# Seven-product FFN: operand making in single steps, one placed behind each block product

## The chip, the cores and the metric

One core of one Trainium2 chip. The metric is the device time of one execution in microseconds, as the median of three runs. The core has TensorE (PE; its weight loads are PEld), VectorE (DVE), ScalarE (ACT), GpSimd (POOL) and SyncE (SP, which here only issues DMAs). Each engine works through its own queue in order.

## What is computed

Three stages in float32: a linear attention over `q`, `k`, `v` (8 x 8 heads, 576 positions, 64 wide), a mixture of eight experts on the 4608 x 512 result, and the feed-forward layer (FFN) that the change is about:

```python
def _moe2_ref(x, w1, w2, w3, w_out):          # x 4608 x 512, w1..w3 512 x 768, w_out 768 x 512
    h = np.maximum(np.maximum(x @ w1, x @ w2), x @ w3)
    return (h @ w_out).astype(np.float32)
```

## The kernel before, in words

The attention and the experts come first and end at about 640 us. The change leaves their work alone, but for the last expert block, in which the first weights of the FFN are made ready.

The FFN takes the tokens in 9 groups of 512. Its first layer makes, for each group, 9 *quads* (class `Quad`, made by `quad1`): three weight columns `fp` by three weights `j`, of which the maximum is taken. Its second layer makes 2 quads for each group (`quad2`). All 81 quads of the first layer run ahead of the 18 of the second. A quad is a 2 x 2 block product done with seven block products in place of eight (numbered 1 to 7; `Quad.step`). For each product both operands must be at hand: blocks of the raw tile as they are (products 1 to 4 on one side or the other) and sums and differences of them. *Sums* of one raw tile are four instructions (`sums_left`, `sums_right`) into a tile `sc`.

float32 runs on TensorE as three matmuls (`mm3`, L482 to L484): each operand is *split* into a high part and the rest (`split`, L797 and L798): ScalarE writes the high part, and VectorE, or in one case GpSimd, subtracts it from the source. A block product of the first layer has 2 x 3 matmuls of 256 columns, of the second 3 x 3. Making the operands of one raw tile is thus: sums (4 instructions), the *single* split (one block, 128 x 256), the *wide* split (two blocks, 128 x 512), and two *pair* splits of the sums (128 x 512 each). There are 9 raw tiles of w1 (a pair of operands for each quad of a group, kept for all groups), 3 of `w_out` (`w2_prep`), 3 of h for each group (`h_steps`, from DRAM), and two halves of x for each group, which first are transposed by TensorE (L1041) into PSUM tiles `tp`.

The order is written out by hand. The last loop runs over the quads n and over the products in the order 6(n), 4(n-1), 1(n+1), 5(n), 7(n), 2(n+1), 3(n); behind each product, `hook(n, p)` may emit other work into the engines' queues. What a product leaves in PSUM (`mm`, six buffers) is taken out at once in the order of emission: products 1, 6 and 5 by a ScalarE copy to `pu` (L1106), since the next product adds onto the same PSUM tile, the others by VectorE (L1091, L1093, L1094, L1116) or ScalarE (L1113) into `mt`. In `hook`:
- `w1_prep` (a generator, `w1_steps`) makes w1 ready from the last expert block on, one step per product; its single and wide splits have GpSimd for the subtraction;
- the operands of x for the next group are made behind four products of quads 6, 7 and 8 of the group;
- the operands of h for the next group are made all at once behind product 1 of the group's first quad: three single, three wide and six pair splits in a row.

Of the kernel before, what the change touches and what calls it, by code (L numbers as in the profile page):

```python
# [45 lines left out]
def kernel(  # L46
# [14 lines left out]
    rt_p = ctx.enter_context(tc.tile_pool(name="rt", bufs=1))  # L61
# [73 lines left out]
    stg_p = []  # L135
    wpools = []
# [369 lines left out]
    ec = ctx.enter_context(ExitStack())  # L506
    with ac:
# [11 lines left out]
        wpools.append(ctx.enter_context(tc.tile_pool(name="wa", bufs=NWA, side="right")))  # L519
        stg_p.append(ctx.enter_context(tc.tile_pool(name="stg", bufs=NSTG, side="right")))  # L520
# [303 lines left out]
    def operand_steps(raw, left, wide, single, whole, half, put, pool, eng=nc.vector):  # L824

        x = [[raw[:, a, b * 256 : (b + 1) * 256] for b in range(2)] for a in range(2)]
        sc = pool.tile([P, 4, 256], F32, name="sc")
        row, names = wide
        if left == "rows":
            sums_left(sc, x[0][0], x[0][1], x[1][0], x[1][1], nc.gpsimd)  # L830
        elif left == "cols":
            sums_left(sc, x[0][0], x[1][0], x[0][1], x[1][1], nc.gpsimd)
        else:
            sums_right(sc, x[0][0], x[0][1], x[1][0], x[1][1], nc.gpsimd)
        h = half()
        split(h, raw[:, 1 - row, single[0] * 256 : (single[0] + 1) * 256], eng)
        put(single[1], h)
        yield
        w = whole()
        split(w, raw[:, row], eng)  # L840
        put(names[0], w[:, :, 0:256])
        put(names[1], w[:, :, 256:])
        yield
        for c, (p, q) in ((0, (6, 7)), (2, (5, 3) if left else (5, 4))):
            w = whole()
            split(w, sc[:, c : c + 2].rearrange("p a b -> p (a b)"))
            put(p, w[:, :, 0:256])
            put(q, w[:, :, 256:])
            yield
# [10 lines left out]
    def w1_steps():  # L860
        half = halves(w1_tile)

        def load(p):
            while conv_done[0] < 2 * p + 2:
                next(conv)
            t = stg_p[0].tile([P, 2, 512], F32, name="stg")
            nc.sync.dma_start(out=t, in_=wfd[2 * p : 2 * p + 2].rearrange("i p c -> p i c"))
            return t

        nxt = load(0)  # L870
        for p in range(9):
            raw, nxt = nxt, load(p + 1) if p < 8 else None
# [151 lines left out]
    xt2_p = fx.enter_context(tc.tile_pool(name="xt2", bufs=18))  # L1024
# [12 lines left out]
    def f_xt(g, i, pool=ps_t, name="tp"):  # L1037
        for k in (i, i + 2):
            ps = pool.tile([P, 4, P], F32, name=name)
            for c in range(4):  # L1040
                nc.tensor.transpose(ps[:, c], xins[g, c // 2][:, c % 2, k * P : (k + 1) * P], ident)  # L1041
            xps[g, k] = ps.rearrange("p c t -> p (c t)")

    def x_new(g, *ps):
        for p in ps:
            for i in range(2):
                xops[g, p, i] = xt2_p.tile([P, 2, 256], F32R, name="xt2")
# [18 lines left out]
    def x_sum(g, n):
        p = (6, 7, 5, 4)[n]
        x_new(g, p)
        for i in range(2):
            x_put(g, p, i, xsc[g, i][:, n])  # L1070
# [93 lines left out]

    w2_half = halves(lambda: wb_p.tile([P, 2, 512], F32R, name="wB"))

    w2_raw = {}

    def w2_load(k):
        w2_raw[k] = stg_p[0].tile([P, 2, 512], F32, name="stg")  # L1170
        nc.sync.dma_start(out=w2_raw[k], in_=wfd[18 + k : 24 : 3].rearrange("i p c -> p i c"))

    def w2_prep(k):
        raw = w2_raw.pop(k)
        w2[k] = {}
        whole = lambda: wb_p.tile([P, 2, 512], F32R, name="wB")
# [247 lines left out]
```

## Time and profile before

| what | value |
|---|---|
| median of 3 runs | 1301.18 us (1300.61 to 1305.65) |
| the profiled execution | 1293.95 us, span 1292.2 us |
| PE busy | 1142.1 us (88%) |
| DVE busy | 833.9 us (65%) |
| ACT busy | 562.7 us (44%) |
| POOL busy | 329.1 us (25%) |
| granted TensorE clock, mean | 0.964 of 2.4 GHz |

The span is from the first to the last instruction. Busy shares are means over stages with different limits, so the stages are looked at by themselves. Where a row names a wait, as in `[3.12 <-ACT pu L1106]`, the engine stood idle for so many us until that instruction was done. A granted clock below 1.00 in a stretch is a mixture of the two levels 2.4 and 1.2 GHz.

### The profile page before, as it was taken

How to read it: one execution, taken by the hardware profiler on the slowest of the kernel's cores; microseconds unless marked ns; L12 is line 12 of the kernel's file. 1: busy time of each engine (PE TensorE's matmuls, PEld its weight loads, DVE VectorE, ACT ScalarE, POOL GpSimd, SP SyncE). 2: the span in 40 equal slices, each digit the busy share in tenths (PEclk: the TensorE clock that was granted, in tenths of full speed). 3: DMA queues.
4: the chain of work that ended last, by engine and by line, in shares of the span. 5: the costliest groups of instructions: out<-in, count | busy, mean ns of one | idle time of the engine just before them, and what ended most of it. 6: DMA issues, size and time to landing. Idle time of an engine off the chain costs nothing.

```text
span 1292.2 us, 34077 instructions
## 1 busy us (share of the span) xinstructions
PE 1142.1 (88%) x14212; PEld 1064.8 (82%) x14212; DVE 833.9 (65%) x1802; ACT 562.7 (44%) x1290; POOL 329.1 (25%) x376
## 2 busy tenths in 40 slices
PE   6999898988786999799878999999999999789886
PEld 6888787877675788688768999999999999678776
DVE  6889688788342677788676565565565668643551
ACT  4665555545431445565453332332332334343441
POOL 0001222204333464441663000000000005535530
PEclk9999999999877999899989999999999999899998
DMA  7576867568523666667421101101201113533411
GB/s 256 190 230 178 215 218 207 169 216 195 107 85 81 220 219 231 231 218 237 164 74 66 66 34 66 66 33 66 65 35 66 55 43 126 183 126 131 156 49 67
DMA packets 115470, 175.84 MB, mean 136 GB/s; under 512 B 20930, under 2 KB 58306, under 8 KB 115312
## 3 DMA queue, kind: packets, MB, share of 16 engines
q1 hardware_dynamic: 110592, 163.63, 39.8%
q0 software_dynamic: 4352, 8.71, 2.0%
q8 instruction: 113, 1.85, 0.6%
q10 hardware_dynamic: 368, 1.27, 0.3%
q14 instruction: 45, 0.37, 0.1%
HBM read 120.77 MB, written 54.78 MB: 136 GB/s over the span
## 4 chain that ended last, share of the span: by engine, by line
PE 59%; DMA 9%; DVE 9%; POOL 8%; issue 7%; ACT 6%; SPq 0%; POOLq 0%; DVEq 0%; ACTq 0%
PE mm L482 13%; PE mm L484 12%; PE mm L483 12%; PE kv L592 6%; PE n L632 5%; PE pr L552 5%; PE tr L569 3%; DMA list<-ids,idx 2%; ACT w L797 2%; DMA xb<-y,ixr 2%; POOL sq L201 1%; PE n L610 1%; PE tp L1041 1%; DMA xb<-y,ix0a 1%; POOL da L202 1%
## 5 line engine op out<-in xcount | busy, mean ns | idle before, releaser
L1106 ACT ACTIVATE pu<-mm 128x256 f32<-128x256 f32 x297 | 112.9, 382 | 244.4 <-PE mm L484 239.4
L482 PE MATMUL mm<-xt,w 128*128 128x256 f32 (+1 forms) x652 | 186.9, 287 | 7.4 <-ACT pu L1106 5.5
L483 PE MATMUL mm<-xt,w 128*128 128x256 f32 (+1 forms) x652 | 186.2, 286 | 1.7 <-DVE xt L478 0.9
L484 PE MATMUL mm<-xt,w 128*128 128x256 f32 (+1 forms) x652 | 186.2, 286 | 0.0
L482 PE MATMUL mm<-xt,wB 128*128 128x256 f32 x536 | 153.9, 287 | 4.0 <-ACT pu L1106 3.6
L483 PE MATMUL mm<-xt,wB 128*128 128x256 f32 x536 | 152.9, 285 | 1.1 <-DVE xt L478 1.1
L484 PE MATMUL mm<-xt,wB 128*128 128x256 f32 x536 | 152.5, 285 | 0.0
L1091 DVE TENSOR_TENSOR mt<-mm,pu 128x256 f32<-128x256 f32 x135 | 56.1, 421 | 121.8 <-PE mm L484 117.9
L482 PEld LDWEIGHTS mm<-xt,w 128*128 128x128 f32 x652 | 125.6, 193 | 8.9 <-ACT pu L1106 6.1
L483 PEld LDWEIGHTS mm<-xt,w 128*128 128x128 f32 x652 | 123.6, 190 | 2.3 <-DVE xt L478 1.2
L1093 DVE TENSOR_TENSOR pu<-mm,pu 128x256 f32<-128x256 f32 x162 | 68.1, 421 | 86.6 <-PE mm L484 86.6
L484 PEld LDWEIGHTS mm<-xt,w 128*128 128x128 f32 x652 | 123.6, 190 | 0.0
L801 POOL TENSOR_TENSOR sc<-stg 128x256 f32<-128x256 f32 x15 | 14.3, 954 | 408.0 <-DMA stg<-hd 377.9
L482 PEld LDWEIGHTS mm<-xt,wB 128*128 128x128 f32 x536 | 103.5, 193 | 5.0 <-ACT pu L1106 4.0
L592 PE MATMUL kv<-raw,e 128*64 128x74 f32 (+1 forms) x2560 | 96.9, 233 | 10.3 <-issue 10.0
L483 PEld LDWEIGHTS mm<-xt,wB 128*128 128x128 f32 x536 | 103.6, 193 | 1.8 <-DVE xt L478 1.8
L592 PEld LDWEIGHTS kv<-raw,e 128*64 128x64 f32 (+1 forms) x2560 | 83.3, 137 | 25.3 <-issue 23.8
L578 ACT ACTIVATE e<-d 128x512 f32<-128x512 f32 x144 | 82.7, 622 | 48.6 <-DVE d L559 46.9
L484 PEld LDWEIGHTS mm<-xt,wB 128*128 128x128 f32 x536 | 103.5, 193 | 0.0
L632 PE MATMUL n<-kvw,q 128*64 128x74 f32 x2304 | 97.0, 236 | 4.7 <-issue 4.0
L552 PE MATMUL pr<-wph,raw 64*64 64x128 f32 x2304 | 85.0, 285 | 12.0 <-DMA wph<-in_w_phi_dram 6.6
L557 DVE TENSOR_REDUCE m<-pr 128x8 f32<-128x1024 f32 x72 | 87.8, 1219 | 10.3 <-PE pr L552 9.3
(250 smaller groups left out, 2953.9 us busy)
## 6 DMA issues: line engine op xcount, KB each, us to landing
raw<-in_qkv_dram SPq DMA_DIRECT2D x46, 798.0 KB, 7.5
stg<-in_w_exp_dram SPq DMA_DIRECT2D x64, 512.0 KB, 5.1
hd<-mt SPq DMA_DIRECT2D x27, 512.0 KB, 3.4
pf<-in_w_ffn_dram SPq DMA_DIRECT2D x24, 512.0 KB, 5.2
hb<-hd SPq DMA_DIRECT2D x21, 512.0 KB, 5.1
xa<-xs SPq DMA_DIRECT2D x16, 576.0 KB, 5.1
xb<-xs SPq DMA_DIRECT2D x16, 576.0 KB, 6.0
stg<-xb SPq DMA_DIRECT2D x18, 512.0 KB, 5.4
```

What stands on the lines that cost most here:

```text
L482: nc.tensor.matmul(out=ps, lhsT=ah, rhs=bh, start=first, stop=False, skip_group_check=on)
L483: nc.tensor.matmul(out=ps, lhsT=ah, rhs=bl, start=False, stop=False, skip_group_check=on)
L484: nc.tensor.matmul(out=ps, lhsT=al, rhs=bh, start=False, stop=last, skip_group_check=on)
L552: nc.tensor.matmul(out=pr[p0 : p0 + 64, h, 2 * s + i], lhsT=raw[k0, o + p0 : o + p0 + 64], rhs=wph[k0], start=True, stop=True,)
L557: nc.vector.tensor_reduce(out=m, in_=pr, axis=AX.X, op=ALU.max, apply_absolute_value=True)
L569: nc.tensor.transpose(tr[:, 2 * h + i], d[:, h, i], ident)
L578: nc.scalar.activation(out=e[:, :, :, s], in_=ds[s2][:, :, 2:4], func=AF.Exp, scale=scale)
L592: nc.tensor.matmul(out=kvps[u, b][c : c + 64, 2 * h + s], lhsT=e[p0:p1, h, i, s, c : c + 64], rhs=v[p0:p1, h], start=t == 4 * b and h + s ...
L632: nc.tensor.matmul(out=ps[p0 : p0 + 64, i, h], lhsT=q[:, s, 2 * h + i, p0 : p0 + 64], rhs=kvw[u, b][:, 2 * h + s], start=s == 0, stop=s == 1,)
L1091: nc.vector.tensor_tensor(out=out, in0=ps, in1=tmp, op=ALU.add)
L1093: nc.vector.tensor_tensor(out=tmp, in0=ps, in1=tmp, op=ALU.add)
L1106: nc.scalar.activation(out=t, in_=ps, func=AF.Copy)
```

## The change

Operand making is cut into single steps: a class `Operands` with the methods `sums`, `single`, `wide`, `pair(0)` and `pair(2)` takes the place of the generator `operand_steps`, and a table `sched` says behind which product (quad n, position `at` in the order above) each step is emitted. `hook` and its conditions are gone.

```diff
-    def operand_steps(raw, left, wide, single, whole, half, put, pool, eng=nc.vector):
...
+    class Operands:
+        def __init__(self, raw, side, whole, half, sums, eng=nc.vector):
+            self.raw, self.side, self.whole, self.half, self.pool, self.eng = raw, side, whole, half, sums, eng
+            self.blocks = {}
+        def steps(self):
+            return [self.sums, self.single, self.wide, lambda: self.pair(0), lambda: self.pair(2)]
...
     def w1_steps():
-        nxt = load(0)
+        cur, nxt = load(0), None
+        yield
+        cur.sums()
         for p in range(9):
-            raw, nxt = nxt, load(p + 1) if p < 8 else None
+            nxt = load(p + 1) if p < 8 else None
             yield
             while w1_used[0] + 4 > (freed[0] - WF + NWA + NWB if not wc_p else NWA + NWB + NWC + 4):
                 yield
-            blocks = {}
-            for _ in operand_steps(raw, "rows", (0, (1, 2)), (1, 4), w1_tile, half, blocks.__setitem__, sc_p, nc.gpsimd):
+            for f in cur.steps()[1:]:
+                f()
                 yield
-            w1[p] = blocks
+                if f == cur.wide and nxt:
+                    nxt.sums()
+            w1[p] = cur.blocks
+            cur = nxt
...
-    xt2_p = fx.enter_context(tc.tile_pool(name="xt2", bufs=18))
+    xB_p = fx.enter_context(tc.tile_pool(name="xB", bufs=12))
+    xT_p = fx.enter_context(tc.tile_pool(name="xT", bufs=8))
...
+    def x_put(g, p, i):
+        if p in (1, 2, 3):
+            t = xB_p.tile([P, 2, 256], F32R, name="xB")
+            split(t, xps[g, i + 2 * (p > 1)][:, 256 * (p == 3) :][:, :256])
+        else:
+            t = xT_p.tile([P, 2, 256], F32R, name="xT")
+            split(t, xsc[g, i][:, (6, 7, 5, 4).index(p)])
+        xops[g, p, i] = t
+    def x_sums(g, i, part=(0, 1)):
+        a, b = xps[g, i], xps[g, i + 2]
+        sub = lambda o, x, y: nc.vector.tensor_tensor(out=o, in0=x, in1=y, op=ALU.subtract)
+        if 0 in part:
+            if g == groups[0]:
+                sc = mt_p.tile([P, 2, 512], F32, name="mt").rearrange("p a (b c) -> p (a b) c", b=2)
+            else:
+                sc = sc_p.tile([P, 4, 256], F32, name="sc")
+            xsc[g, i] = sc
+            nc.scalar.activation(out=sc[:, 3], in_=a[:, 256:], func=AF.Copy)
+            sub(sc[:, 2], sc[:, 3], a[:, 0:256])
+            sub(sc[:, 0], b[:, 256:], sc[:, 2])
+        if 1 in part:
+            sc = xsc[g, i]
+            sub(sc[:, 1], b[:, 256:], sc[:, 3])
+            sub(sc[:, 3], b[:, 0:256], sc[:, 0])
...
+    ORDER = (6, 4, 1, 5, 7, 2, 3)
+    def do(n, at, f, *args):
+        sched.setdefault((n, ORDER[at]), []).append((f, args))
...
+    def x_next(n0, g):
+        do(n0 + 3, 6, f_load, g)
+        for i in range(2):
+            q = n0 + 5 + i
+            do(q, 0, f_ps, g, i)
+            do(q, 0, f_xt, g, i)
+            for at, p in ((2, 1), (3, 2), (4, 3)):
+                do(q, at, x_put, g, p, i)
+            do(q, 5, x_sums, g, i, (0,))
+            do(q, 6, x_sums, g, i, (1,))
+        for i in range(2):
+            do(n0 + 8, 1 + i, x_put, g, 6, i)
+            do(n0 + 8, 4 + i, x_put, g, 5, i)
+            do(n0 + 8 + i, 6 * (1 - i), x_put, g, 7, i)
+            do(n0 + 9, 2 + i, x_put, g, 4, i)
...
+    def h_next(n0, i):
+        if i + 2 < NG:
+            for k in range(3):
+                do(n0, 1, h_load, groups[i + 2], k, hb_p, "hb", sb_p)
+        if i + 1 < NG:
+            g = groups[i + 1]
+            for k in range(3):
+                do(n0, 1, op_step, h_op, (g, k), 0)
+            at = [(n0 + (2 + t) // 7, (2 + t) % 7) for t in range(12)]
+            for s, first in ((1, 0), (2, 3), (3, 6), (4, 9)):
+                for k in range(3):
+                    do(*at[first + k], op_step, h_op, (g, k), s)
...
+    for n in range(5):
+        for at in range(7):
+            do(n, at, next, w1_prep, None)
+    do(5, 0, list, w1_prep)
...
-            hook(n, p)
+            for f, args in sched.pop((n, p), ()):
+                f(*args)
```

The steps for the second layer's first group (`to_layer2`) are placed one by one too: three tiles of h from quad 74 on, three of w_out from quad 77 to 80, where they were made a tile at a time behind quads 75 to 80. Besides: `sb` (sums of h) has 4 buffers and not 3; h is loaded two groups ahead and not three; pools are opened in another order, so that tiles lie at other addresses; the first x group is transposed in two halves, the two token halves of all its tiles one after the other, and its two loads stand behind four loads of w1 in SP's queue and not behind five.

On ScalarE in the second layer, from one copy `pu` (L1106, L1124 after) to the next but a group, there stood before:

```order
L1106 ACTIVATE pu<-mm 128x256 x2
L797 ACTIVATE w<-hb 128x256 x3
L797 ACTIVATE w<-hb 128x512 x3
L797 ACTIVATE w<-sc 128x512 x6
L1106 ACTIVATE pu<-mm 128x256
L1113 ACTIVATE mt<-mm 128x256
```

and there stand after:

```order
L795 ACTIVATE w<-hb 128x256
L1124 ACTIVATE pu<-mm 128x256
L795 ACTIVATE w<-hb 128x256 x2
L795 ACTIVATE w<-hb 128x512
L1131 ACTIVATE mt<-mm 128x256
L795 ACTIVATE w<-hb 128x512
L1124 ACTIVATE pu<-mm 128x256
L795 ACTIVATE w<-hb 128x512
L795 ACTIVATE w<-sc 128x512
L1124 ACTIVATE pu<-mm 128x256
L795 ACTIVATE w<-sc 128x512
L1124 ACTIVATE pu<-mm 128x256
```

The twelve splits that stood between two copies are dealt out between the copies of two quads.

On GpSimd at the start of the FFN, behind the last scatter of expert rows (`xb<-y`), before:

```order
L951 DMA xb<-y,ixr_8323 3456x512
L801 TENSOR_TENSOR sc<-stg 128x256
L802 TENSOR_TENSOR sc<-sc,stg 128x256
L803 TENSOR_TENSOR sc<-stg 128x256
L804 TENSOR_TENSOR sc<-stg,sc 128x256
L798 TENSOR_TENSOR w<-stg,w 128x256
L798 TENSOR_TENSOR wB<-stg,wB 128x512
```

and after:

```order
L802 TENSOR_TENSOR sc<-stg,sc 128x256
L966 DMA xb<-y,ixr_8323 3456x512
L799 TENSOR_TENSOR sc<-stg 128x256
L800 TENSOR_TENSOR sc<-sc,stg 128x256
L801 TENSOR_TENSOR sc<-stg 128x256
L802 TENSOR_TENSOR sc<-stg,sc 128x256
```

The two subtractions of each w1 tile (single and wide) have left GpSimd for VectorE, and the sums of one more tile stand ahead of the scatter.

On VectorE in quad 5 of a group of the first layer (behind products 7, 2 and 3, in which the next group's x is begun; `tp` is the transposed x), after:

```order
L1111 TENSOR_TENSOR pu<-mm,pu 128x256
L1112 TENSOR_TENSOR mt<-mt,pu 128x256
L796 TENSOR_TENSOR xB<-tp,xB 128x256
L1109 TENSOR_TENSOR mt<-mm,pu 128x256
L1075 TENSOR_TENSOR sc<-sc,tp 128x256
L1075 TENSOR_TENSOR sc<-tp,sc 128x256
L1134 TENSOR_TENSOR mt<-mm,mt 128x256
L1075 TENSOR_TENSOR sc<-tp,sc 128x256 x2
```

where before the same stood in one piece in quad 6:

```order
L1116 TENSOR_TENSOR mt<-mm,mt 128x256
L798 TENSOR_TENSOR xt_10638<-tp,xt_10638 128x256
L798 TENSOR_TENSOR xt_10640<-tp,xt_10640 128x256
L807 TENSOR_TENSOR sc<-sc,tp 128x256
L808 TENSOR_TENSOR sc<-tp,sc 128x256
```

The four differences that stood together behind product 6 now stand two and two behind products 2 and 3 of the quad before.

## Rows read from the trace of the kernel before

**Rows 1.** Stretches: span, busy PE, PEld, DVE, ACT, POOL (count), clock, DMA, GB/s.
```profile
655.40:693.70 38.30, 30.57 (x206) 29.16 (x207) 27.58 (x41) 17.63 (x42) 34.69 (x36) 0.87 0.22 70
707.00:756.00 49.00, 47.20 (x397) 46.79 (x396) 28.62 (x73) 16.63 (x47) 0.00 (x0) 1.00 0.16 55
1102.60:1142.90 40.30, 27.68 (x215) 27.07 (x213) 25.18 (x42) 17.90 (x41) 20.34 (x25) 0.87 0.41 145
1142.90:1258.30 115.40, 96.57 (x756) 95.35 (x756) 53.83 (x109) 51.30 (x120) 56.79 (x72) 0.94 0.34 118
1258.30:1281.00 22.70, 22.62 (x189) 22.42 (x189) 5.17 (x12) 4.60 (x12) 0.00 (x0) 1.00 0.19 71
```

**Rows 2.** Waits, 707 to 1062: who for whom, total us, times, longest.
```profile
PE mm L482 <- ACT pu L1106: 8.6, 8, 1.1
PE tp L1041 <- DVE xt L798: 5.8, 8, 0.7
```

**Rows 3.** Waits, 1102.6 to the end.
```profile
PE mm L482 <- ACT pu L1106: 31.0, 8, 9.1
DVE mt L1091 <- DMA out_dram<-mt: 3.8, 3, 1.8
```

**Rows 4.** Timeline, 1139 to 1143, three engines and PE: start, us, instruction.
```profile
1139.40 3.22 ACT L797 ACTIVATE w<-sc 128x512 fp32r<-128x512 f32 x6
1140.31 3.70 DVE L798 TENSOR_TENSOR w<-sc,w 128x512 fp32r<-128x512 f32 x6
1142.52 0.37 ACT L1106 ACTIVATE pu<-mm 128x256 f32<-128x256 f32 x1
1142.88 1.72 POOL L801 TENSOR_TENSOR sc<-hb 128x256 f32<-128x256 f32 x1 [11.06 <-DVE w L798]
1142.94 0.39 PE L482 MATMUL mm<-wB,wC 128*128 128x256 f32 x1 [3.12 <-ACT pu L1106]
```

**Rows 5.** Stretches behind two of the eight waits.
```profile
1162.80:1169.00 6.20, 6.18 (x54) 6.18 (x55) 2.17 (x5) 1.54 (x4) 6.04 (x8) 1.00 0.62 231
...
1180.80:1187.00 6.20, 6.15 (x39) 6.15 (x40) 2.20 (x5) 0.88 (x3) 6.04 (x8) 0.72 0.42 150
```

**Rows 6.** Groups by line and form, 1124 to 1281: busy us, mean ns, idle before.
```profile
L1091 DVE TENSOR_TENSOR mt<-mm,pu 128x256 f32<-128x256 f32 x52 | 21.3, 422 | 78.7 <-PE mm L484 74.9 <-DMA out_dram<-mt 3.8
...
L803 POOL TENSOR_TENSOR sc<-hb 128x256 f32<-128x256 f32 x21 | 15.4, 736 | 0.0
L798 DVE TENSOR_TENSOR w<-sc,w 128x512 fp32r<-128x512 f32 x24 | 14.8, 684 | 0.0
...
L797 ACT ACTIVATE w<-hb 128x512 fp32r<-128x512 f32 x18 | 10.1, 622 | 0.0
...
L798 DVE TENSOR_TENSOR w<-hb,w 128x256 fp32r<-128x256 f32 x21 | 7.7, 421 | 9.5 <-ACT w L797 9.5
```

**Rows 7.** Timeline, 1111 to 1116, VectorE and GpSimd; first and last of five sums.
```profile
1111.39 4.93 DVE L798 TENSOR_TENSOR w<-stg,w 128x256 fp32r<-128x256 f32 x5 [0.71 <-ACT w L797]
1111.96 0.92 POOL L804 TENSOR_TENSOR sc<-stg,sc 128x256 f32<-128x256 f32 x1
...
1115.73 1.19 POOL L804 TENSOR_TENSOR sc<-stg,sc 128x256 f32<-128x256 f32 x1
```

**Rows 8.** Groups by line and form, VectorE, 656 to 692.
```profile
L798 DVE TENSOR_TENSOR wB<-sc,wB 128x512 fp32r<-128x512 f32 x6 | 8.3, 1403 | 5.1 <-ACT wB L797 5.1
```

**Rows 9.** Groups by line and form, VectorE, 1064 to 1104.
```profile
L1094 DVE TENSOR_TENSOR mt<-mt,pu 128x256 f32<-128x256 f32 x16 | 9.4, 587 | 0.6
...
L798 DVE TENSOR_TENSOR w<-sc,w 128x512 fp32r<-128x512 f32 x6 | 3.8, 681 | 0.0
```

**Rows 10.** Timeline of the start of the FFN, TensorE and GpSimd.
```profile
646.54 1.54 PE L1041 MATMUL tp<-ident,stg 128*128 128x128 f32 x6 [2.73 <-DMA stg<-xb]
655.46 0.39 PE L482 MATMUL mm<-xt,w 128*128 128x256 f32 x1 [3.35 <-ACT pu L1106]
656.08 0.85 POOL L801 TENSOR_TENSOR sc<-stg 128x256 f32<-128x256 f32 x1 [10.59 <-DVE xt L798]
```

More of the change, by code (lines that the diff above doesn't have):

```diff
@@ L822, in halves, with sums, single, wide @@
         return half
-    def operand_steps(raw, left, wide, single, whole, half, put, pool, eng=nc.vector):
[L826 to L849, printed above, removed]
+    class Operands:
[4 more added lines that the diff above has]
+            return [self.sums, self.single, self.wide, lambda: self.pair(0), lambda: self.pair(2)]
+        def sums(self):
+            r = self.raw
+            x = [[r[:, a, b * 256 : (b + 1) * 256] for b in range(2)] for a in range(2)]
+            self.sc = self.pool.tile([P, 4, 256], F32, name="sc")
+            if self.side == "rows":
+                sums_left(self.sc, x[0][0], x[0][1], x[1][0], x[1][1], nc.gpsimd)
+            elif self.side == "cols":
+                sums_left(self.sc, x[0][0], x[1][0], x[0][1], x[1][1], nc.gpsimd)
+            else:
+                sums_right(self.sc, x[0][0], x[0][1], x[1][0], x[1][1], nc.gpsimd)
+        def single(self):
+            h = self.half()
+            rows = self.side == "rows"
+            split(h, self.raw[:, 1, 256:] if rows else self.raw[:, 0, 0:256], self.eng)
+            self.blocks[4 if rows else 1] = h
+        def wide(self):
+            w = self.whole()
+            split(w, self.raw[:, 0 if self.side == "rows" else 1], self.eng)
+            a, b = {"rows": (1, 2), "cols": (2, 4), "right": (2, 3)}[self.side]
+            self.blocks[a], self.blocks[b] = w[:, :, 0:256], w[:, :, 256:]
+        def pair(self, c):
+            w = self.whole()
+            split(w, self.sc[:, c : c + 2].rearrange("p a b -> p (a b)"))
+            a, b = (6, 7) if c == 0 else (5, 4) if self.side == "right" else (5, 3)
+            self.blocks[a], self.blocks[b] = w[:, :, 0:256], w[:, :, 256:]
@@ L1035, in f_load, with f_ps @@
             xins[g, c] = t
-    def f_xt(g, i, pool=ps_t, name="tp"):
+    def f_ps(g, i, pool=ps_t, name="tp"):
         for k in (i, i + 2):
[L1039 to L1047, printed above, removed]
@@ L1066, in x_sum, with f_xt @@
[L1066 to L1070, printed above, removed]
+            xps[g, k] = pool.tile([P, 512], F32, name=name)
+    def f_xt(g, i, cs=range(4)):
+        for k in (i, i + 2):
+            for c in cs:
+                nc.tensor.transpose(
+                    xps[g, k][:, c * P : (c + 1) * P], xins[g, c // 2][:, c % 2, k * P : (k + 1) * P], ident
+                )
+    def x_put(g, p, i):
[6 more added lines that the diff above has]
+        xops[g, p, i] = t
@@ new lines @@
+    for i in range(2):
+        x_sums(g0, i, (0,))
+    for i in range(2):
+        x_put(g0, 6, i)
+    for i in range(2):
+        x_sums(g0, i, (1,))
+    for p in (5, 7, 3, 4):
+        for i in range(2):
+            x_put(g0, p, i)
+    quads = [(quad1, g, p) for g in groups for p in range(9)] + [(quad2, g, m) for g in groups for m in range(2)]
+    for n in range(5):
+        for at in range(7):
+            do(n, at, next, w1_prep, None)
+    do(5, 0, list, w1_prep)
+    for i in range(1, NG):
+        x_next(9 * (i - 1), groups[i])
@@ L1224 @@
+    to_layer2(NQ1 - 9)
+    do(NQ1, 1, layer2_pools)
+    for i in range(NG):
+        h_next(NQ1 + 2 * i, i)
     made = {}
```

176 lines of the change are left out of this document (59 added, 117 removed), and 6 rows, old and new, of the table q.

## The prediction

> **What bounds the kernel now.** The share of busy time over the whole span hides where TensorE stands still, so the table of stretches is read first [rows 1]: length, busy time and number of instructions of each engine, the granted clock. Its last row is a stretch in which nothing waits: 189 matmuls in 22.7 us, 0.120 us each at full clock (2.4 GHz). A block product of the first FFN layer has 6 matmuls (0.72 us), of the second 9 (1.08 us); a quad of seven products takes 5.04 and 7.56 us. Measured against that price:
> - Second layer, 1102.6 to 1258.3: 40.3 + 115.4 = 155.7 us for 215 + 756 = 971 matmuls, which need 116.5 us. Lost: 39.2 us.
> - First quads of the first layer, 655.4 to 693.7: 38.3 us for 206 matmuls, which need 24.7 us. Lost: 13.6 us.
> - Steady first layer: 49.0 us hold nine quads (45.4 us) and 16 transposes of x. The waits there [rows 2] are 8.6 + 5.8 = 14.4 us at eight changes of group, 1.8 us each.
>
> Then the waits of the second layer [rows 3]: TensorE waits 8 times, 31.0 us together and once 9.1 us, for one ScalarE copy, `pu` at L1106. The timeline of one of them [rows 4] shows that the copy is not late by its own input: six splits of `hb` and then six of `sc` stand ahead of it in ScalarE's queue, it runs at 1142.52, and TensorE starts again at 1142.94 after 3.12 us. VectorE's half of the splits lies there too, and only behind it does GpSimd begin the sums of the next group, which then run alone. So no engine is full; three engines take turns. After such a wait the clock may be at the lower level for a while [rows 5]: 6.2 us hold 54 matmuls at 1.00 and only 39 at 0.72, 15 x 0.120 = 1.8 us. That is part of the 39.2.
>
> **Second layer.** A group is two quads, 126 matmuls, 15.1 us. The change adds no instruction here; it deals the twelve splits of the next group out, one behind a product, and the sums go ahead of all of them. Prices of one group [rows 6]: VectorE 3 x 0.42 + 9 x 0.684 = 7.4 us of splits and 6 x 0.42 = 2.5 us of sums of products, 9.9 us; GpSimd 12 sums x 0.74 = 8.9 us; ScalarE about the same as VectorE (a split 0.62). All are below 15.1 us, and the order shows at most three splits between two copies, one behind each product, so a copy stands behind one split of 0.62 us that came a product before it, where twelve stood. Product 6 overwrites what the copy of product 1 reads only five products later, 5 what 6 left three later, so that 0.62 us has 2 x 1.08 us to hide in.
>
> New is that sums and splits run side by side. Where they do so before [rows 7], five sums (0.92 to 1.19 us, not 0.74) and five splits (4.93 us, alone about 2.6) alternate from 1111.4 to 1116.3: each sum holds a split up by (4.93 - 2.6) / 5 = 0.46 us. Twelve sums can cost VectorE at most 12 x 0.46 = 5.5 us a group, 15.4 against 15.1 us, so the bounds are 0 and 0.3 x 8 = 2.4 us, and I take 1. All eight waits and the slow clock behind them go: 39.2 - 1 = **38 us** (bounds 32, if a wait of 0.8 us stays in each group, and 41). What is late next is VectorE, on `sc`. The two `mt` buffers come round faster; VectorE waited 3.8 us in 3 waits for the output DMA [rows 3], and a quad of 7.56 us still leaves four products, 4.3 us, between a DMA's issue and the next write, so I cost it at nothing.
>
> The Trainium skill (SBUF — State Buffer, section "SBUF: two separate sides") says that a VectorE instruction with two SBUF inputs and a GpSimd one exclude each other for the whole instruction. The rows show alternation but a hold of 0.46 us, less than the 0.74 us that a sum takes; by the page the hold would be all of it. What that would give is the first rival.
>
> **Change of group in the first layer.** The steps of x that came in four lumps are spread over quads 5 to 9. Of the 1.8 us, 1.07 was the copy behind lumps on ScalarE [rows 2]; what ScalarE now has ahead of a copy waits for differences that VectorE made quads before, so that goes. The other 0.72 us was a transpose waiting for VectorE to let go of a `tp` buffer, and it stays in another form: the second set of transposes stands right behind product 6 of quad 6, and its second half needs a buffer that VectorE's last two differences read, which the order puts behind the maximum of product 3. From the end of product 7 VectorE has nine instructions of 0.42 us, 3.8 us; TensorE needs 3 x 0.72 + 4 transposes of about 0.1 = 2.6 us for products 2, 3, 6 and the first transposes. About 0.8 us is left, down to 0 if the first three start early, up to 1.2. Gain 1.0 us x 8 = **8 us** (bounds 3 and 14).
>
> **Start of the FFN.** Three edits. First, `lo` of the single and wide splits of w1 goes from GpSimd to VectorE. Before, GpSimd is busy 34.7 of the 38.3 us [rows 1]: six sets of four sums and two splits, one set each 6 us, and five quads go at that pace, 38.3 x 210 / 206 = 39 us. With 24 sums alone GpSimd has 24 x 0.74 to 0.92 = 18 to 22 us. VectorE now has 6 x 0.42 + 18 x 0.684 = 14.8 us of splits and, in quads 0 to 4, 27 instructions of products at 0.42, 11.3 us: 26 us against 25.2 us of TensorE, plus up to 24 x 0.46 = 11 us of holds. The nearest stretch with just this mix, sums on GpSimd and all splits on VectorE, is 1064 to 1104 [rows 9]: splits of 512 at 0.681 and only the SBUF-only maximum stretched, 0.587; in the stretch of the entry itself, with GpSimd's own long splits, VectorE's took 1.40 [rows 8]. I take the first: 29 to 31 us for five quads, 8 to 10 us less. Second, the sums of the first x group go to `mt`, so that GpSimd, which waited 10.59 us for VectorE to free `sc` [rows 10], goes on; that is in the pace above. Third, the x loads come one w1 load earlier in SP's queue: the transposes' second wait of 2.73 us for the DMA can go, but VectorE's 22 steps of x (22 x 0.42 = 9.2 us) still stand ahead of the first copy, for which TensorE waited 3.35 us until 655.46 [rows 10]. I count 1 us. Moved past nothing else: SP's order otherwise is the same. Together **10 us** (bounds 0 and 16).
>
> **Last nine quads of the first layer.** The same 24 splits start 1.3 quads earlier, at quad 74 and not 75. VectorE was full there before and is about full now (14.8 us + 6 quads of 2.4 us = 29 us and holds, against 30 us): 0, bounds -2 and +2. All up to the last expert block stays as it is; three more splits of VectorE there lie beside matmuls: 0.
>
> Sum: 38 + 8 + 10 = 56 us. The profiled execution took 1293.95 us (span 1292.2), so 1238 us for one like it. The runs' median was 1301.18 us, 7.2 us above it; I take the 56 us off that: **1245 us**.
>
> **Rivals.**
> 1. *Whole-instruction exclusion.* Sums and splits share one place: 8.9 + 7.4 = 16.3 us a group, 1.2 us above 15.1, 9.6 us in eight groups. At the entry a set takes 4 x 0.74 = 3.0 us of sums, 2.5 of splits and 0.6 of the maximum (two SBUF inputs as well), six 36 us, which leaves 3 of the 39 and so costs 7 us of my gain; in the last nine quads the same 36 us stand against six quads, 30 us: 6 us. Gain 56 - 23 = 33: 1268 us. This is the rule of the Trainium skill's page named above. For it: rows 7 do alternate. Against it: the hold there is 0.46. Chance 0.11.
> 2. *Late sums.* The split of the third `h` tile's first sums stands nine products behind the sums' start, 9.7 us, and needs eleven sums: 8.1 us at 0.74, 10.2 at 0.93, 13.1 at 1.19 (all rows 6 and 7). At 1.19 ScalarE waits 3.4 us, 1.2 more than the 2.2 that the copies have to spare, and what VectorE does behind it as much again: 2.4 us x 8 = 19 us. Gain 37: 1264 us. Chance 0.09.
> 3. *Slower: GpSimd becomes the bound.* The longest sum of the trace took 1.72 us [rows 4], where splits stood against it. If all did, a group took 12 x 1.72 = 20.6 us against 115.4 / 6 = 19.2 before: 11 us worse in the second layer; 24 x 1.72 = 41 us at the entry (2 worse than 39) and 41 against 30 in the last nine quads (11 worse), less 8 at the changes of group: 16 us slower, 1317 us. It begins to bind at 15.1 / 12 = 1.26 us a sum and loses from about 1.65. Against it: sums in the mix of rows 7 took at most 1.19. Chance 0.04.
> 4. *It does not do what it says*, the splits still bunch and the times cancel: 1301 us. The order shows them apart. Chance 0.03.
>
> **How the numbers follow.** My forecast has 0.73, and its own bounds give 1232 to 1258; rival 2 lies at 1264, 1 at 1268. The range 1230 to 1264 leaves out rivals 1, 3 and 4 and a little of the forecast, about 2 in 10. A measurement of this kernel can tell about 0.5% (6.5 us) from no change: faster 0.93, same 0.03, slower 0.04.
>
> **What would show it.** Right: in the second layer no wait of TensorE for the `pu` copy above 1 us, the clock at 1.00, and 126 matmuls in 15 to 15.5 us; VectorE's 512 splits between 0.7 and 1.0; at the entry GpSimd below 25 us and five quads in some 30 us; at each change of group one wait of under 1 us, for VectorE. Wrong: sums above 1.3 us, ScalarE waiting for sums for over 2 us, VectorE full in the second layer, or a clock below 1.00 without waits ahead of it.

## The result and the profile after

On the chip the kernel after took 1256.89 us (median of 1252.49, 1254.32, 1259.46 and 1259.92), the kernel before, beside it, 1300.89 us: a ratio of 0.966 with a 95% interval of 0.961 to 0.971, 44 us less. The forecast was 1245 us and 56 us less, with a range of 1230 to 1264. So the direction was right, the time lies inside the range, and 12 us of the forecast gain are missing. The profiled execution took 1259.92 us (span 1258.0).

First the table of stretches, cut so that a stretch holds the same matmuls in both kernels: up to the last expert matmul; to the 210th FFN matmul (five quads; the rest of the nine, up to the next cut, is not shown); seven groups of the steady first layer; its last nine quads; the second layer. Columns: stretch, length, busy time and count of PE, PEld, DVE, ACT, POOL, clock, DMA share, GB/s. Before:

```profile
0.00:640.50 640.50, 564.87 (x9531) 495.82 (x9532) 460.41 (x956) 319.52 (x659) 194.61 (x217) 0.96 0.63 193
640.50:692.20 51.70, 34.68 (x229) 32.25 (x228) 36.76 (x60) 24.05 (x60) 38.19 (x40) 0.88 0.31 97
716.90:1059.60 342.70, 330.14 (x2761) 327.25 (x2760) 200.35 (x512) 116.11 (x324) 0.00 (x0) 1.00 0.16 55
1059.60:1106.20 46.60, 45.70 (x380) 45.09 (x379) 39.15 (x81) 22.65 (x58) 19.19 (x24) 1.00 0.40 136
1106.20:1280.80 174.60, 143.60 (x1136) 141.94 (x1134) 80.90 (x154) 71.29 (x167) 77.13 (x96) 0.93 0.34 118
```

The same stretches after:

```profile
0.00:660.90 660.90, 574.27 (x9532) 502.83 (x9532) 467.23 (x962) 319.76 (x659) 189.96 (x213) 0.95 0.62 187
660.90:705.60 44.70, 33.40 (x228) 31.81 (x227) 38.80 (x73) 24.33 (x60) 22.35 (x26) 0.85 0.41 123
728.90:1066.20 337.30, 328.97 (x2761) 326.29 (x2760) 199.72 (x513) 114.86 (x323) 0.00 (x0) 1.00 0.16 56
1066.20:1112.80 46.60, 45.34 (x380) 44.94 (x379) 39.72 (x81) 23.36 (x58) 21.06 (x24) 1.00 0.40 137
1112.80:1246.80 134.00, 134.00 (x1136) 134.00 (x1134) 97.41 (x155) 72.20 (x167) 89.86 (x96) 1.00 0.45 154
```

Read the second column from the bottom. The second layer fell by 40.6 us and is now busy for 134.0 of its 134.0 us at full clock; the last nine quads stayed; seven groups fell by 5.4 us, 0.77 a group; the first five quads with what leads to them by 7.0 us. From the last expert matmul to the last matmul it is 640.2 us before (640.5 to 1280.7) and 585.9 us after (660.9 to 1246.7): 54.3 us less, of 56 forecast. But the first row is 20.4 us longer, in a stage for which the forecast had 0.

The waits of TensorE in the whole FFN after (who for whom, total us, times, longest) answer to [rows 2, 3]:

```profile
PE tp L1060 <- DVE sc L1075: 9.5, 16, 1.0
PE mm L483 <- ACT pu L1124: 4.7, 1, 4.7
PE mm L483 <- DVE pu L1111: 4.1, 2, 3.4
PE tp L1060 <- DMA stg<-xb: 2.4, 1, 2.4
PE mm L483 <- DVE mt L1109: 1.0, 2, 0.5
PE tp L1060 <- DVE xB L796: 0.3, 1, 0.3
```

TensorE had waited 31.0 us for the `pu` copy (now L1124) in the second layer alone [rows 3]; now it waits for it once in the whole FFN, at the entry. The largest group now are sixteen waits at the eight changes of group.

What took the place of [rows 4] is seen on ScalarE's timeline in the second layer (start, us, instruction, idle before and what ended it):

```profile
1152.35 0.38 ACT L1124 ACTIVATE pu<-mm 128x256 f32<-128x256 f32 x1 [0.15 <-PE mm L485]
1152.63 0.62 ACT L795 ACTIVATE wC<-hb 128x512 fp32r<-128x512 f32 x1
1153.15 0.62 ACT L795 ACTIVATE wC<-sc 128x512 fp32r<-128x512 f32 x1
1154.46 0.39 ACT L1124 ACTIVATE pu<-mm 128x256 f32<-128x256 f32 x1 [0.69 <-PE mm L485]
```

Two splits stand between two copies, and the second copy waits for its product, not the product for it. Where twelve splits stood in a row, it is now ScalarE that waits for TensorE.

Groups by line and form from 1108 to 1228 (busy us, mean ns, idle before) answer to [rows 6, 7]; the last line is the stretch behind them:

```profile
L796 DVE TENSOR_TENSOR wC<-sc,wC 128x512 fp32r<-128x512 f32 x24 | 22.5, 960 | 0.4 <-ACT wC L795 0.2
...
L801 POOL TENSOR_TENSOR sc<-hb 128x256 f32<-128x256 f32 x21 | 21.8, 1037 | 0.0
...
L799 POOL TENSOR_TENSOR sc<-hb 128x256 f32<-128x256 f32 x21 | 17.2, 819 | 17.3 <-DVE wC L796 6.6 <-DVE w L796 5.9 <-DMA hb<-hd 4.8
...
L796 DVE TENSOR_TENSOR w<-hb,w 128x512 fp32r<-128x512 f32 x18 | 14.5, 808 | 6.1 <-ACT w L795 6.0
L795 ACT ACTIVATE wC<-sc 128x512 fp32r<-128x512 f32 x24 | 14.1, 623 | 0.4 <-POOL sc L801 0.4
```
```profile
1229.00:1246.00 17.00, 17.00 (x146) 17.00 (x146) 6.52 (x13) 6.06 (x14) 0.00 (x0) 1.00 0.25 94
```

Sums and splits do slow each other: in the means of these groups 0.82 to 1.04 us a sum instead of 0.74, 0.81 to 0.96 us a split of 512 instead of 0.68. TensorE waits for none of it, and ScalarE for sums 0.4 us in all.

### The profile page after: what moved, and what is told of

Read it like the earlier page. It is cut to its first block, busy times and chain, and to the rows that moved or that the text cites. A ratio compares the mean times of both kernels' runs of the same rounds, so it can differ in the third digit from the quotient of the medians.

```text
span 1258.0 us, 34053 instructions
## 1 busy us (share of the span) xinstructions
PE 1138.3 (90%) x14212; PEld 1061.6 (84%) x14212; DVE 858.8 (68%) x1820; ACT 563.4 (45%) x1290; POOL 323.2 (26%) x358
## 4 chain that ended last, share of the span: by engine, by line
PE 68%; DMA 9%; DVE 7%; issue 7%; POOL 5%; ACT 2%; SPq 0%; POOLq 0%; ACTq 0%; DVEq 0%
PE mm L485 15%; PE mm L483 15%; PE mm L484 15%; PE kv L590 6%; PE n L630 6%; PE pr L550 6%; PE tr L567 3%; DMA list<-ids,idx 2%; PE n L608 1%; DMA xb<-y,ixr 1%; DMA xb<-y,ix0a 1%; PE tp L1060 1%; DVE sc L1075 1%; POOL sq L202 1%; POOL da L203 1%
## 5 line engine op out<-in xcount | busy, mean ns | idle before, releaser
L1124 ACT ACTIVATE pu<-mm 128x256 f32<-128x256 f32 x297 | 114.3, 385 | 270.9 <-PE mm L485 261.3
L630 PEld LDWEIGHTS n<-kvw,q 128*64 128x64 f32 x2304 | 87.7, 143 | 16.2 <-issue 13.6
L202 POOL TENSOR_TENSOR sq<-sq,pf 128x512 f32<-128x512 f32 x24 | 31.8, 1323 | 238.3 <-DVE pf L200 196.8
L557 DVE TENSOR_TENSOR d<-pr,m 128x1024 f32<-128x1024 f32 x72 | 88.2, 1224 | 4.9 <-ACT sq L185 0.5
L483 PE MATMUL mm<-xT,w 128*128 128x256 f32 x288 | 81.8, 284 | 9.1 <-ACT pu L1124 4.7
L569 ACT ACTIVATE q<-tr 128x512 f32<-128x512 f32 x72 | 42.8, 595 | 103.6 <-PE tr L567 95.2
L550 PEld LDWEIGHTS pr<-wph,raw 64*64 64x64 f32 x2304 | 67.6, 139 | 22.2 <-issue 16.4
L1109 DVE TENSOR_TENSOR mt<-mm,pu 128x256 f32<-128x256 f32 x135 | 56.2, 416 | 39.1 <-PE mm L485 38.6
L484 PE MATMUL mm<-xT,w 128*128 128x256 f32 x288 | 81.4, 282 | 0.0
L485 PE MATMUL mm<-xT,w 128*128 128x256 f32 x288 | 81.3, 282 | 0.0
L1112 DVE TENSOR_TENSOR mt<-mt,pu 128x256 f32<-128x256 f32 x162 | 71.7, 443 | 5.6
L484 PE MATMUL mm<-wB,w 128*128 128x256 f32 x266 | 74.6, 280 | 0.0
L485 PE MATMUL mm<-wB,w 128*128 128x256 f32 x266 | 74.5, 280 | 0.0
L483 PE MATMUL mm<-wB,w 128*128 128x256 f32 x266 | 74.4, 280 | 0.0
```

The source lines that it names most:

```text
L483: nc.tensor.matmul(out=ps, lhsT=ah, rhs=bh, start=first, stop=False, skip_group_check=on)
L484: nc.tensor.matmul(out=ps, lhsT=ah, rhs=bl, start=False, stop=False, skip_group_check=on)
L485: nc.tensor.matmul(out=ps, lhsT=al, rhs=bh, start=False, stop=last, skip_group_check=on)
L550: nc.tensor.matmul(out=pr[p0 : p0 + 64, h, 2 * s + i], lhsT=raw[k0, o + p0 : o + p0 + 64], rhs=wph[k0], start=True, stop=True,)
L557: nc.vector.tensor_tensor(out=d, in0=pr, in1=m[:, :, :, None].to_broadcast([P, 2, 4, P]), op=ALU.subtract)
L630: nc.tensor.matmul(out=ps[p0 : p0 + 64, i, h], lhsT=q[:, s, 2 * h + i, p0 : p0 + 64], rhs=kvw[u, b][:, 2 * h + s], start=s == 0, stop=s == 1,)
```

## Experiments

Two questions were open: whether each term of the FFN is due to the edit that it was put down to, and where 12 us (44 against 56) and the 20 us of the first stage come from. In what follows "FFN" is the time from the last expert matmul to the last matmul of a profile. The kernels of one paragraph were not all run on one chip; each ratio is against the kernel before on the same chip.

**The stage ahead of the FFN.** The kernel before once more, and before with nothing but the new places of the pools:

> The kernel before once more, for a second profile of its attention and experts. In the profiled executions the last expert matmul came at 640.5 us before and at 660.9 us after, though the order of instructions up to there is the same. Spread theory: executions of one program differ by this much, and the two profiles fell at opposite ends; then it comes somewhere between 640 and 660 us here, by chance. Layout theory: the new places of the pools in SBUF slow the first 640 us; then it stays at 640 to 645 us, as in the first profile. The FFN behind it takes 640 us again by both (640.5 to 1281.0).

> The kernel before with the new places of the pools alone (expert weights, staging, routing tables and constants), all FFN steps as before. Spread theory: no difference, ratio 1.000 with an interval that holds 1, last expert matmul between 640 and 660 us by chance. Layout theory: 10 to 12 us slower, the part of the forecast gain that did not come (56 forecast, 44 measured), ratio about 1.009, last expert matmul at 651 to 661 us. FFN 640 us by both.

> The kernel before with the new places of the pools alone, once more, beside the kernel before. Its instructions, their order and their waits are those of before, and only the addresses in SBUF differ. Layout theory: the ratio 1.0049 (1.0017 to 1.008) of the first measurement comes again, interval above 1. Spread theory: it was chance, and the interval holds 1 here, or lies below.

```diff
-    rt_p = ctx.enter_context(tc.tile_pool(name="rt", bufs=1))
+    wpools = [ctx.enter_context(tc.tile_pool(name="wa", bufs=NWA, side="right"))]
+    stg_p = [ctx.enter_context(tc.tile_pool(name="stg", bufs=NSTG, side="right"))]
+    ec = ctx.enter_context(ExitStack())
+    rt_p = ec.enter_context(tc.tile_pool(name="rt", bufs=1, side="right"))
...
-    upper = const.tile([P, P], BF16, name="upper")
+    upper = rt_p.tile([P, P], BF16, name="upper")
```

The new places cost 0.49% (0.17 to 0.80; medians 1297.01 and 1291.78 us) and on another chip 0.39% (0.14 to 0.65; 1309.03 and 1305.21 us): about 5.7 us, twice with an interval above zero, and only half of what the layout theory asked for. Engine by engine this kernel and the kernel before hold the same instructions in the same order with the same waits; only addresses in SBUF differ. And the kernel after again:

> The kernel after once more, beside the kernel before on the same chip. Spread theory: the 660.9 us up to the last expert matmul in its first profile was one slow execution, and it comes between 640 and 650 us here, as in the four other profiles taken since; the ratio to before is then 1 - 54/1292 = 0.958 to 0.960. Layout theory, in the size that the kernel with the new places alone showed (1.0049 with 1.0017 to 1.008): 48 us of gain, ratio 0.962 to 0.966. FFN 586 us by both (660.9 to 1246.7 in the first profile).

> The kernel after, beside the other three on this chip, as the base of their differences. By the first two measurements 0.961 to 0.966 of before; FFN 586 us.

> The other half of the second layer's change undone: the splits stay dealt out one behind a product as in the kernel after, but the four sums of each h tile go to GpSimd three products ahead of the split that needs them, and not all twelve ahead of the first split. Theory (GpSimd needs its early start, since twelve sums of 0.96 us take 11.5 of the 15.1 us of a group): the second and third tile's splits come 1.5 and 4 us after their place, ScalarE and VectorE wait for GpSimd and TensorE for them, 2 to 3 us a group, 16 to 24 us more than the kernel after. Rival, that dealing out alone is enough: less than 6 us more.

```diff
-            for k in range(3):
-                do(n0, 1, op_step, h_op, (g, k), 0)
...
                     do(*at[first + k], op_step, h_op, (g, k), s)
+                    if s == 2:
+                        do(*at[first + k], op_step, h_op, (g, k), 0)
```

The last of these was meant as an experiment on the sums and is none. GpSimd's queue in the second layer holds the sums and nothing else, in the same order; where in the program they are written moves no instruction on any engine, and the two kernels are one and the same. Its result is therefore a third repeat of the kernel after, and the question (must the sums be early?) was not tested. The ratios are 0.961 (0.957 to 0.965), 0.963 (0.960 to 0.967) and 0.963 (0.959 to 0.968). With the first, 0.966, their mean is 0.963: 48 us of 1301. The first repeat ended its first stage at 658.3 us, where the spread theory had expected 640 to 650.

The first stage in the profiles, same table, one row each. In this order: before again, new places, new places again, after again, after a third time, and the repeat with the sums written later:

```profile
0.00:644.20 644.20, 570.03 (x9531) 500.11 (x9532) 461.80 (x956) 319.00 (x659) 195.17 (x217) 0.95 0.63 192
```
```profile
0.00:645.10 645.10, 567.46 (x9532) 497.83 (x9532) 463.07 (x956) 320.14 (x659) 193.60 (x217) 0.96 0.62 192
```
```profile
0.00:648.60 648.60, 573.35 (x9531) 501.22 (x9532) 461.92 (x956) 319.51 (x659) 192.42 (x217) 0.96 0.62 191
```
```profile
0.00:658.30 658.30, 573.55 (x9531) 501.79 (x9532) 466.94 (x962) 319.16 (x659) 190.24 (x213) 0.95 0.62 187
```
```profile
0.00:658.60 658.60, 571.43 (x9531) 499.24 (x9532) 466.38 (x962) 319.53 (x659) 190.34 (x213) 0.96 0.62 187
```
```profile
0.00:651.20 651.20, 571.49 (x9531) 500.44 (x9532) 467.44 (x962) 319.18 (x659) 189.38 (x213) 0.96 0.62 189
```

The last two are the same instructions on the same chip, 7.4 us apart; the four profiles of the kernel after lie between 651.2 and 660.9 us, those of before at 640.5 and 644.2. Two kernels further down, the one with the second layer's steps in one lump (its first form) and the one with the x steps in lumps, hold the same instructions as the kernel after up to this point, with the new places too:

```profile
0.00:640.30 640.30, 563.64 (x9531) 494.86 (x9532) 467.04 (x962) 319.26 (x659) 189.73 (x213) 0.96 0.62 193
```
```profile
0.00:644.10 644.10, 566.48 (x9531) 495.66 (x9532) 466.60 (x962) 319.43 (x659) 191.67 (x213) 0.97 0.62 192
```

So one and the same first stage took from 640.3 to 660.9 us, as much as the whole difference between the first two profiles; the second of these rows is from the same chip as the 658.6 and the 651.2. The FFNs of the four profiles of the kernel after are 585.9, 586.0, 586.6 and 586.2 us, and with the old steps (before twice, the new places twice) 640.2, 640.2, 640.1 and 640.5. So nearly all the scatter of this kernel is in its first stage, and the 20 us are scatter, in which the two profiles happened to fall apart, with the smaller cost of the places in it. That cost can be read from the other kernels as well: for each of the ten measurements of a kernel with the new places and the new steps, its median less that of before on its chip, less what its FFN differs from 640.2 us, gives between -1.5 and 10.3 us, 5.1 in the mean.

Of TensorE's idle time, the part that goes with the scatter is that in which it waited for nothing that the profile shows ("issue"). Up to 640 us, summed over the lines, it is 23.3 and 22.3 us before, 25.3 and 26.1 with the new places, 28.4 to 36.7 in the four profiles of the kernel after, and 23.7 and 25.4 in the two short ones just shown: it goes with the length of the stage in that execution, not with the places. Why addresses should change the time, and what the scatter is, stays open.

**The second layer.** The sums and splits of a group in one lump again, in two forms of writing:

> The kernel after with the second layer's sums and splits of a group in one lump again, behind the second product of a group, in the order of before; the rest as after. Turns theory (engines took turns, and dealing the steps out was worth 38 to 41 us): 1257 + 38 to 41 = 1295 to 1298 us, eight waits of about 4 us of TensorE for the pu copy come back. Rival (the fourth buffer of sb, the lump one product earlier, or the fuller clock gave a good part): 1270 to 1285 us.

> The kernel after with half of the second layer's change undone: GpSimd's sums of a group start ahead of all splits, as after, but the twelve splits stand in one lump behind the second product of a group. Theory that it is the dealing out that counts: the pu copies stand behind twelve splits on ScalarE, the last of them behind the twelfth sum, 12 x 0.96 = 11.5 us later; about the 45 us of the full lump (FFN 631 us against 586) stay lost, 35 us at least. Rival, that the early start of the sums is what counts: less than 15 us is lost.

```diff
-            at = [(n0 + (2 + t) // 7, (2 + t) % 7) for t in range(12)]
-            for s, first in ((1, 0), (2, 3), (3, 6), (4, 9)):
+            for s in (1, 2, 3, 4):
                 for k in range(3):
-                    do(*at[first + k], op_step, h_op, (g, k), s)
+                    do(n0, 2, op_step, h_op, (g, k), s)
```

The two are again one program, for the same reason as above, so they are one experiment run twice. (The diff is that of the second form.) Ratios 0.999 (0.996 to 1.002) and 1.001 (0.997 to 1.004), 3.7 and 3.9% above the kernel after; FFN 631.1 and 632.0 us, 45 to 46 us more. The second layer of the first of them, and its waits for the copy:

```profile
1092.00:1271.50 179.50, 147.44 (x1136) 144.71 (x1134) 93.16 (x155) 71.31 (x167) 82.28 (x96) 0.91 0.33 115
```
```profile
PE mm L483 <- ACT pu L1124: 31.0, 8, 9.0
```

It is [rows 3] once more to the digit, 31.0 us in eight waits, with the clock at 0.91. The turns theory holds, and its rival (a fourth buffer of `sb` does part of it) falls: that buffer is there, and the loss is even 5 us larger than before. The early start of the sums alone brings nothing either: in the first form the sums of one group end at 1137.5 us and its splits begin on VectorE only at 1143.0, and all eight waits are there. Whether the dealing out needs the early sums is not shown.

**The entry.** The second half of the raw w1 splits on GpSimd again:

> The kernel after with the second half of the w1 splits of raw weights (single and wide) on GpSimd again. In the two profiles the time from the last expert matmul to the 210th matmul of the FFN fell from 51.7 to 44.7 us, 7 us. Theory that GpSimd's own long splits set the pace of the first quads: 1257 + 5 to 8 us, GpSimd busy for over 33 us there, VectorE's 512 splits back at 1.2 to 1.4 us. Rival (the x steps at the entry and VectorE's queue set it): 1257 within 2 us, since VectorE loses 12 splits and gains nothing else to wait for.

```diff
-            return Operands(t, "rows", w1_tile, half, sc_p)
+            return Operands(t, "rows", w1_tile, half, sc_p, nc.gpsimd)
```

Ratio 0.967 (0.962 to 0.972), FFN 592.5 us, 6.5 us more than after. The stretch up to the 210th FFN matmul, TensorE's waits in it, and one group of GpSimd's from 648 to 692:

```profile
641.30:692.60 51.30, 34.41 (x228) 31.77 (x227) 35.11 (x58) 24.41 (x60) 38.60 (x41) 0.83 0.36 108
```
```profile
PE mm L483 <- ACT pu L1124: 12.1, 4, 7.0
```
```profile
L796 POOL TENSOR_TENSOR wB<-stg,wB 128x512 fp32r<-128x512 f32 x3 | 4.8, 1608 | 0.8 <-ACT wB L795 0.8
```

51.3 us beside 51.7 before and 44.7 after, and GpSimd busy for 38.6 of them: undoing this one edit takes nearly the whole 7.0 us of that stretch back. VectorE's splits of sums there take 1.28 to 1.42 us again, as expected. In the times the 6.5 us lie at the edge of what can be told.

**The change of group.** The x steps in lumps again, and, the other way, the second set of transposes two products later:

> The kernel after with the x steps of a group in four lumps again (load half a quad later, first and second set of transposes with their splits and differences behind product 6 of quad 6 and the maximum of quad 7's end, the splits of the sums in two lumps and a rest in quad 8). Theory: the changes of group cost 1.8 us again and not the 0.95 + 0.24 of the profile after and its pipeline gaps; 8 x 0.8 = 6 us more than the kernel after (5 to 8). Rival, that the lumps fit here because VectorE has room in the steady quads: 0 to 2 us more.

> The kernel after with the second set of transposes of a group, and the steps that hang on it, two products later. In the profile after TensorE waits 0.95 us eight times for VectorE to let go of a tp buffer ahead of these transposes and 0.24 us ahead of the first set. Theory of the prediction (the order stands them too soon behind the first set): the 0.95 goes, 8 x 0.95 = 7.6 us less than the kernel after. Rival: what VectorE does later then meets the next quads, and 4 us or more of it comes back as waits for mt, pu or xB.

```diff
-        do(n0 + 3, 6, f_load, g)
+        do(n0 + 4, 0, f_load, g)
         for i in range(2):
-            q = n0 + 5 + i
...
+            q = (n0 + 6 + i, 6 * i)
...
+            do(*q, f_xt, g, i)
+            do(*q, x_put, g, 1, i)
+            do(*q, x_put, g, 2, i)
+            do(*q, x_sums, g, i)
...
+        for q, p in (((n0 + 8, 0), 6), ((n0 + 8, 6), 5), ((n0 + 8, 6), 7), ((n0 + 9, 2), 4)):
+            for i in range(2):
+                do(*q, x_put, g, p, i)
```
```diff
             q = n0 + 5 + i
-            do(q, 0, f_ps, g, i)
-            do(q, 0, f_xt, g, i)
+            do(q, 2 * i, f_ps, g, i)
+            do(q, 2 * i, f_xt, g, i)
             for at, p in ((2, 1), (3, 2), (4, 3)):
-                do(q, at, x_put, g, p, i)
-            do(q, 5, x_sums, g, i, (0,))
-            do(q, 6, x_sums, g, i, (1,))
+                do(q, at + 2 * i, x_put, g, p, i)
+            do(q + i, 5 * (1 - i), x_sums, g, i, (0,))
+            do(q + i, 6 - 5 * i, x_sums, g, i, (1,))
```

The first of these diffs is that of the lumps, the second that of the later set. With the lumps, seven groups and the waits of all eight changes:

```profile
713.20:1055.00 341.80, 329.32 (x2760) 326.43 (x2759) 200.91 (x511) 115.50 (x323) 0.00 (x0) 1.00 0.16 55
```
```profile
PE mm L483 <- ACT pu L1124: 8.5, 8, 1.1
PE tp L1060 <- DVE xB L796: 5.7, 8, 0.7
```

The very waits of [rows 2] are back, 8.5 and 5.7 us (8.6 and 5.8 there), and the FFN is 591.5 us, 5.1 us more than after. The times don't show it: 0.963 (0.960 to 0.967), the same as after on that chip. Its six runs lie between 1248.9 and 1262.6 us, and a first stage that scatters by more than 5 us hides such a term. It is read from its own stage or not at all here.

The second set later: 0.956 (0.952 to 0.960), 1243.90 us beside 1253.92 us of the kernel after on the same chip; FFN 574.4 us, 11.6 us less. Its seven groups:

```profile
721.10:1048.40 327.30, 327.30 (x2760) 326.24 (x2760) 199.22 (x512) 113.84 (x323) 0.00 (x0) 1.00 0.17 57
```

337.3 us became 327.3, with TensorE busy all the time. Expected were 7.6 us, from the 0.95 us wait. The 0.25 us one ahead of the first set went too, 9.5 us for both in the profile after; the other 2 us stand in no wait of the profile.

**Both.** The entry rearranged as well:

> As the kernel with the second set later, and at the start of the FFN the first product of quad 0 goes ahead of the sums of x, and the splits of x for the later products are put behind products, so that the pu copy of that product doesn't stand behind twelve splits on ScalarE (TensorE waited 4.66 us there in the profile after). Theory: 2 to 4 us less than the kernel with the second set later. Rival: the same splits are then waited for one by one, and it is the same within 1 us.

The move of the second set, shown above, and the lines taken away further up are left out:

```diff
...
     step(0, 1)
-    step(0, 2)
+    for i in range(2):
+        x_sums(g0, i, (0,))
...
+    for at, p in ((0, 5), (1, 4), (2, 7), (2, 3)):
+        for i in range(2):
+            do(0, at, x_put, g0, p, i)
+    do(0, 3, step, 0, 2)
```

0.956 (0.952 to 0.960), FFN 573.7 us, 0.7 us less, no more than the scatter of an FFN: the rival holds. Waits at the entry:

```profile
PE mm L483 <- ACT xT L795: 3.9, 1, 3.9
```

The copy no longer stands behind the splits, but the next product needs the split of a sum of x, and that chain (copies on ScalarE, four differences on VectorE, two splits) takes the time whatever stands beside it. The kernel with the second set later is the simplest version that beats both kernels.

## Why the prediction was right, and where its sum was off

- **Second layer, 38 forecast, 40.6 measured.** The mechanism is shown: the lump alone brings the eight waits and the clock back. The step that was too careful is the 1 us for sums and splits holding each other. VectorE's busy time in the layer rose from 80.9 to 97.4 us, 16.5 / 96 = 0.17 us a sum and not up to 0.46, 2.1 us a group and not 5.5; VectorE is at 73%. Also a matmul costs 134.0 / 1134 = 0.118 us, not 0.120.
- **Rival 1, exclusion for the whole instruction.** It asked for 16.3 us a group, 130 us for eight. All eight groups' sums and splits run from 1116.3 to 1234.9 us (GpSimd's last sum ends at 1225.3), 118.7 us or 14.8 a group; GpSimd and VectorE overlap. Where they meet they do hold each other: of the second layer's splits of 512, the 48 that had a sum beside them for at least half of their time took 1.01 us in the mean, the 22 that had none 0.68. The Trainium skill (SBUF — State Buffer, section "SBUF: two separate sides") states such an exclusion for instructions with two SBUF inputs; the 14.8 us a group, below 16.3, disagree with its full length, and the measurement decides here.
- **Rival 2, late sums.** In the first group it came close: the eleventh sum ends at 1126.51 us, and ScalarE had waited 0.4 us for it, its only wait for a sum in the layer. But the sums took 0.82 to 1.04 us in the mean, below the 1.19 that it supposed, and they don't wait for their place in the program: from the fourth group on GpSimd begins them 10 us ahead of the group's first split, and from the second on the eleventh is ready 2.4 to 6.5 us before it is needed. **Rival 3** needed 1.26 us. **Rival 4**: the splits do stand apart.
- **Change of group, 8 forecast, 6.2 measured** (0.77 x 8). The place was right, the size a little off: left over are

```profile
713.29 0.63 PE L1060 MATMUL tp<-ident,stg 128*128 128x128 f32 x4 [0.25 <-DVE sc L1075]
...
714.87 0.63 PE L1060 MATMUL tp<-ident,stg 128*128 128x128 f32 x4 [0.95 <-DVE sc L1075]
```

  which is 1.2 us and not the 0.8 that I took: 0.95 for the second set, near what was forecast, and 0.25 for the first, which the step did not have.
- **Start of the FFN, 10 forecast, about 7.6 measured** (from the last expert matmul to the first of the FFN and from there to the 378th, 8.9 + 67.5 us before and 6.0 + 62.0 after, 8.4 less, of which 0.8 is the change of group in it). The x part gave 1.9 us (1 forecast). The pace from the first unhindered product to the 210th matmul fell from 36.7 to 31.7 us, 5 us; forecast were 8 to 10. The step that failed is "I take the first [rows 9]". VectorE from 667 to 705:

```profile
L796 DVE TENSOR_TENSOR wB<-sc,wB 128x512 fp32r<-128x512 f32 x6 | 4.1, 717 | 0.6 <-ACT wB L795 0.6
...
L796 DVE TENSOR_TENSOR wB<-stg,wB 128x256 fp32r<-128x256 f32 x4 | 3.7, 926 | 0.0
...
L796 DVE TENSOR_TENSOR wB<-stg,wB 128x512 fp32r<-128x512 f32 x3 | 3.1, 1046 | 1.1 <-ACT wB L795 1.1
```

  In these groups the splits of sums cost 0.72 us, but those of raw weights 1.05 and 0.93 us, not 0.68 and 0.42. What decides is not what a split reads, but whether a sum runs on GpSimd at the same time. Two splits of raw weights from the entry, the first while GpSimd stood idle, the second beside a sum:

```profile
677.85 0.69 DVE L796 TENSOR_TENSOR wB<-stg,wB 128x512 fp32r<-128x512 f32 x1 [1.07 <-ACT wB L795]
...
688.18 0.91 POOL L802 TENSOR_TENSOR sc<-stg,sc 128x256 f32<-128x256 f32 x1
688.42 1.22 DVE L796 TENSOR_TENSOR wB<-stg,wB 128x512 fp32r<-128x512 f32 x1
```

  The row that the step took was not of the mix that it was taken for: none of the six splits of [rows 9] had a sum beside it. Other groups of the same stretch of the kernel before, 1064 to 1104, showed the hold already:

```profile
L798 DVE TENSOR_TENSOR w<-stg,w 128x512 fp32r<-128x512 f32 x3 | 2.6, 867 | 0.1
...
L798 DVE TENSOR_TENSOR wB<-stg,wB 128x256 fp32r<-128x256 f32 x3 | 2.4, 797 | 0.0
```

  VectorE was busy for 38.8 of 44.7 us at the entry, and TensorE waits 3.4 us for it at 694.65. GpSimd stayed below 25 us, as forecast (22.35).
- **Last nine quads, 0 forecast, 0.0 measured.**
- **All up to the last expert block, 0 forecast: wrong.** That sentence looked at instructions and queues, which indeed are the same, and not at the pools, whose new places cost about 5.7 us in two measurements and 5.1 us in the mean of ten more. With it the parts close: 54.3 - 5.7 = 48.6 us, beside 48 us in the mean of four. The 44 us of the first measurement and its 12 missing us are that and scatter.
- **The base.** The forecast took the median of the runs, 1301.18 us; in four measurements before took 1300.9, 1291.8, 1305.2 and 1305.2 us.

## What to carry to other kernels

When engines take turns and none is full, deal the side work out behind the main work in pieces no longer than the slack of a buffer, and price the result by the stretch in which nothing waits. Before a price is taken from a stretch, look at whether the neighbour that may hold the instruction ran there at the same time. Ask of every edit which queue it changes: an instruction written at another place in the program moves only if it passes another instruction of its own engine. Where one stage of a kernel scatters by more than an edit is worth, read the edit from the stage that it touches, and take repeats for the rest.

## What was not expected of the hardware

- The FFN repeats to 0.7 us in four profiles of the kernel after (585.9 to 586.6), while the same instructions ahead of it took from 640.3 to 660.9 us in six profiles; the kernel before took 1281.5 to 1300.4 us on a single chip.
- The same instructions, order and waits with other addresses in SBUF took 0.39 and 0.49% longer. Which of the moved pools does it, and how, was not tried.
- VectorE's splits of 512 took 0.68 us with no sum on GpSimd beside them, whether they read a raw tile or finished sums, and 1.22 us in the mean of the five at the entry that had one for at least half of their time. In turn a sum of 0.74 us took up to 1.2 us beside splits.
